# Attention with running sums: sums first, three heads fed from SBUF, and a new order of VectorE's and GpSimd's work

## The chip, the core and the metric

The kernel runs on one core of a Trainium2 chip. Its engines are named as in the profile: PE (TensorE, matrix products), PEld (its weight loads), DVE (VectorE), ACT (ScalarE), POOL (GpSimd) and SP (SyncE, which issues most of the DMAs). Each engine works through a queue of its own in order and waits on semaphores for the others. SBUF is the on-chip memory, PSUM the memory that PE writes its products to. The metric is the time of one execution on the device in microseconds (us). It is taken several times, and the median counts.

## The reference

Attention with a causal mask and a bias made of running sums, and behind it two gated MLPs whose input is the attention's output:

```python
# q, k, v: (4, 8, 576, 64), s: (4, 8, 576)
scores = (1 / sqrt(64)) * q @ k.T
cum = cumsum(maximum(s, 0), -1)
bias = -(cum[..., :, None] - cum[..., None, :])
scores = where(causal, -1e9, scores + minimum(bias, 0))
attn = exp(scores - max(scores))
attn = attn / (sum(attn) + 1e-9)
x = (attn @ v), heads side by side        # 2304 x 512
x = (sigmoid(x @ w_gate) * (x @ w_val)) @ w_out        # d_ff 1536
x = ((x @ w_a) * (x @ w_b)) @ w_out2                   # d_ff 1536
```

## The kernel before

There are 32 heads, i = 0 to 31. Each has 576 rows in 5 chunks and 64 columns. Values are split into a high part, rounded to fp32r, and a low part, the exact rest, so that products of parts come near to fp32.

**Tiles of a head.** `r` (3 buffers) holds q in one half of the partitions and k in the other. `o` (4 buffers) holds the high parts of both, and below them the rows that add the bias: the running sums `relk` and `relq`, selector rows of constants, and the row of maxima. `o2` (3 buffers) holds high and low parts for the second product. `rel` is the SBUF tile with the running sums of all heads, split in high and low. `pt` are the exponentials, `xt` the output before it is divided, `rb` the reciprocals spread over 64 partitions, `x_sb` the attention's output.

**Steps of a head, with engine and line.** Load r (SP L337). High parts: q on POOL (`hq1`, L465), k on ACT (`hk1`, L467). Copies of the high parts into `o2` by DMA: k issued by ACT (`hk2`, L468), q by SP (`hq2`, L469). Low parts by subtraction on DVE: `lok` (L470) and `loq` (L472). Loads of the head's running sums into `o` (`rel`, SP L476, L477) from DRAM copies `relk_d` and `relq_d`. Scores in two halves, S(i,0) and S(i,1) (PE L492, with the mask by L497). Both go to the same PSUM tile `ps_g`, so the second can't start before the maxima of the first, and S(i+1,0) not before those of S(i,1). Maxima on DVE (L505): `mx0` of the first half, `mx1` of the second. Their transpose on PE (mT, L512), a copy on ACT (L514) and a DMA into `o` (L516). Scores again, transposed and with the maxima taken off: ST (PE L529, L530). Exponentials on ACT (`ex`, L535). The causal cut on POOL (`cs`, three affine_selects, L551). The product with v, where columns of ones give the row sums (pv, PE L564). Copy to `xt` (ACT L573), the sums' DMA (L575), reciprocals for two heads at once (`rc`, DVE L588 and L589), their way through DRAM (`rd` L597, `rb` L594), and the final product on POOL (`xm`, L577).

**MLP weights** are split beside attention, one tile of 128x512 about every three heads: ACT L224 and L243, DVE L225, L227, L229, L232, and `wr` on POOL (L244).

**Start.** `s` is loaded, broadcast to 4 times 32 rows (L400). DVE sets tiles to constants (L346 to L356), then makes the sums (L403 to L408), ACT rounds them (`relh`, L417), DVE makes their rest (`rell`, L418). Head 0 gets its sums from SBUF: `relk` by SP (L431), `relq` by four DMAs of POOL (L424). All sums are stored to DRAM (`relq_d` by POOL L429, `relk_d` by SP L436), and heads 1 to 31 load theirs from there.

**What sets the order.** Every step is registered with `op(name, engine, cost, function, needs, prio)`. `emit(in_order=True)` takes, among the steps whose needs are already emitted, the one with the lowest `prio`. So `prio`, a time in nominal us in which a head takes HT = 6.1, sets the order of each engine's queue, and nothing else does: costs and latencies are not used, and each engine runs its queue in that order. On PE a period reads S(n,0), ST(n-2), S(n,1), pv(n-3), mT(n), S(n+1,0).

Hardware DMAs take eight semaphores in turn. A DMA waits for the one that had its semaphore before.

Of the kernel before, what the change touches and what calls it, by code (L numbers as in the profile page):

```python
# [119 lines left out]
def attn_mlp_kernel(  # L120
# [169 lines left out]
    def attention():  # L290
        with ExitStack() as c2:
# [58 lines left out]
            for e in range(2):  # L350
                nc.vector.memset(vx_t[e][:, :, (1 - e) * D:(2 - e) * D], 1.0)
                nc.vector.memset(vx_t[e][TL:128, 4, e * D:(e + 1) * D], 0.0)
            for t in nm_t:
                nc.vector.memset(t, 0.0)
            for t in pt_t:
                nc.vector.memset(t[TL:128, P0[4]:], 0.0)  # L356
# [60 lines left out]
            op("relh", "ACT", 0.67, lambda: nc.scalar.copy(out=rel[:, 0], in_=cum), ["sums"], -100)  # L417
            op("rell", "DVE", 0.7, lambda: nc.vector.tensor_tensor(  # L418
                out=rel[:, 1], in0=cum, in1=f32(rel[:, 0]), op=ALU.subtract), ["relh"], -100)


            def relq(c):
# [17 lines left out]
            for j in range(1, NO):  # L440
                if j < NR2:
                    op(("lqk", j), "SP", 0.6, lambda j=j: load_qk(j), [("sel", j - 1)], -90 + j, lat=3.0)
                op(("sel", j), "SP", 1.3, lambda j=j: selectors(o_t[j]), [("lqk", j)], -60 + j, lat=2.2)
# [374 lines left out]
```

## Time and profile before

| | |
|---|---|
| median of 3 runs | 1170.98 us (1170.71 to 1171.28) |
| the profiled execution: its own time | 1173.02 us |
| its span in the trace | 1171.3 us |
| PE busy | 1112.4 us (95%) |
| DVE busy | 648.3 us (55%) |
| ACT busy | 335.5 us (29%) |
| POOL busy | 314.5 us (27%) |
| mean granted clock of PE | 0.993 of full speed |

The span runs from the first to the last record of the trace; the execution's own time lies 1.7 us above it. The attention fills the first quarter of the span; the MLPs behind it keep PE at 90% or more of nearly every slice. Shares are means over both parts, so the shares of DVE and POOL within the attention are far above those in the table.

### The profile page before, as it was taken

What the parts mean: (1) busy time and instruction counts of PE and PEld (TensorE: products, weight loads), DVE (VectorE), ACT (ScalarE), POOL (GpSimd) and SP (SyncE); (2) the same over time, 40 slices, a digit from 0 to 9 for tenths busy, and PEclk for the clock granted to TensorE, in tenths of its full rate; (3) what the DMA queues carried; (4) which work ended last, traced back from release to release, by engine and by line L of the source; (5) the groups of instructions that cost most, each with busy time, mean ns of one, the idle gap of its engine ahead of it and who ended that gap; (6) DMA issues with size and microseconds to landing.
All of it is one profiled execution on the core that took longest, in us unless ns stands there. A gap on an engine that the chain in (4) does not pass through costs nothing.

```text
span 1171.3 us, 16041 instructions
## 1 busy us (share of the span) xinstructions
PE 1112.4 (95%) x6152; PEld 1043.9 (89%) x6152; DVE 648.3 (55%) x1016; ACT 335.5 (29%) x603; POOL 314.5 (27%) x395
## 2 busy tenths in 40 slices
PE   1799898999999999999999999999999999999998
PEld 0677777788999999999999999899999999999997
DVE  4588888846422595335873348732478333753322
ACT  1345455443322342112421123422243111321100
POOL 3146655554200242001430023311134110311100
PEclk9999999998999999999999999999999999999999
DMA  3466566723200131001220003300033000200001
GB/s 91 121 164 158 149 169 162 162 63 100 72 2 1 50 113 55 1 1 37 91 90 1 1 18 98 101 1 1 2 93 108 15 1 1 72 27 27 28 28 54
DMA packets 69730, 74.07 MB, mean 63 GB/s; under 512 B 28549, under 2 KB 53293, under 8 KB 69654
## 3 DMA queue, kind: packets, MB, share of 16 engines
q1 hardware_dynamic: 66518, 68.09, 20.3%
q10 hardware_dynamic: 2880, 4.80, 1.9%
q8 instruction: 49, 0.80, 0.3%
q14 instruction: 27, 0.22, 0.1%
q0 software_dynamic: 256, 0.15, 0.0%
HBM read 57.70 MB, written 5.60 MB: 54 GB/s over the span
## 4 chain that ended last, share of the span: by engine, by line
PE 72%; DVE 15%; DMA 4%; issue 3%; POOL 2%; ACT 2%; SPq 0%; ACTq 0%; POOLq 0%; DVEq 0%
PE ps L277 22%; PE ps L278 22%; PE ps L276 22%; PE ps_x L564 3%; DVE nm L505 3%; DVE u L227 2%; PE ps_g L492 1%; DVE raw L229 1%; DVE u L225 1%; DVE raw L232 1%; DVE o L472 1%; DMA r<-in_qk_dram 1%; POOL w L244 1%; DVE h L710 1%; DVE hf L696 1%
## 5 line engine op out<-in xcount | busy, mean ns | idle before, releaser
L276 PE MATMUL ps<-xs,w 128*128 128x384 f32 x1152 | 385.1, 334 | 0.0
L278 PE MATMUL ps<-xs,w 128*128 128x384 f32 x1152 | 385.0, 334 | 0.0
L277 PE MATMUL ps<-xs,w 128*128 128x384 f32 x1152 | 384.9, 334 | 0.0
L707 POOL TENSOR_SCALAR h<-hf 128x384 fp32r<-128x384 f32 x144 | 91.7, 637 | 577.1 <-DVE hf L696 577.1
L696 DVE TENSOR_TENSOR hf<-ps,g 128x384 f32<-128x384 f32 x144 | 79.9, 555 | 281.3 <-PE ps L278 281.2
L276 PEld LDWEIGHTS ps<-xs,w 128*128 128x128 f32 x1152 | 216.3, 188 | 0.7
L277 PEld LDWEIGHTS ps<-xs,w 128*128 128x128 f32 x1152 | 216.3, 188 | 0.7
L278 PEld LDWEIGHTS ps<-xs,w 128*128 128x128 f32 x1152 | 216.2, 188 | 0.0
L692 ACT ACTIVATE g<-ps 128x384 f32<-128x384 f32 x144 | 70.7, 491 | 437.6 <-PE ps L278 437.6
L244 POOL TENSOR_TENSOR w<-raw,w 128x512 fp32r<-128x512 f32 x72 | 100.4, 1396 | 131.8 <-ACT w L243 129.3
L710 DVE TENSOR_TENSOR h<-hf,h 128x384 fp32r<-128x384 f32 x144 | 88.9, 617 | 83.5 <-POOL h L707 83.5
L276 PE MATMUL ps<-h,w 128*128 128x384 f32 x288 | 97.9, 340 | 2.2 <-POOL h L707 2.1
L278 PE MATMUL ps<-h,w 128*128 128x384 f32 x288 | 97.6, 339 | 2.1 <-POOL w L244 2.1
L564 PE MATMUL ps_x<-pt,vx 128*128 128x320 f32 (+4 forms) x448 | 97.3, 370 | 1.1 <-ACT xt L573 0.9
L277 PE MATMUL ps<-h,w 128*128 128x384 f32 x288 | 97.6, 339 | 0.6 <-DVE h L710 0.6
L505 DVE TENSOR_REDUCE nm<-ps_g 128x1 f32<-128x512 f32 (+4 forms) x160 | 77.0, 530 | 35.0 <-PE ps_g L497 34.9
L564 PEld LDWEIGHTS ps_x<-pt,vx 128*128 128x128 f32 x448 | 77.2, 194 | 18.9 <-ACT xt L573 1.5
L277 PE MATMUL ps<-w,h 128*128 128x512 f32 x216 | 84.6, 392 | 1.0 <-POOL w L244 0.9
L278 PE MATMUL ps<-w,h 128*128 128x512 f32 x216 | 84.4, 391 | 0.0
L276 PE MATMUL ps<-w,h 128*128 128x512 f32 x216 | 84.1, 389 | 0.0
L492 PE MATMUL ps_g<-o 128*128 128x512 f32 (+2 forms) x192 | 45.9, 350 | 35.0 <-POOL o L465 18.8
L243 ACT CAST w<-raw 128x512 fp32r<-128x512 f32 x72 | 47.1, 657 | 101.5 <-DVE raw L232 95.6
(90 smaller groups left out, 1346.5 us busy)
## 6 DMA issues: line engine op xcount, KB each, us to landing
raw<-in_moe_w_out_dram SPq DMA_DIRECT2D x24, 512.0 KB
r<-in_qk_dram SPq DMA_DIRECT2D x32, 288.0 KB
raw<-in_moe_w_gate_dram SPq DMA_DIRECT2D x12, 512.0 KB
raw<-in_moe_w_val_dram SPq DMA_DIRECT2D x12, 512.0 KB
raw<-in_moe_w_a_dram SPq DMA_DIRECT2D x12, 512.0 KB
raw<-in_moe_w_b_dram SPq DMA_DIRECT2D x12, 512.0 KB
o<-o ACTq DMA_DIRECT2D x32, 144.0 KB
o<-o SPq DMA_DIRECT2D x32, 144.0 KB
```

Of the source, the lines that this page charges most:

```text
L243: ("ACT", 0.53, lambda: nc.scalar.copy(out=wtile(n, m)[:, 0], in_=value())),
L244: ("Pool", 1.23, lambda: nc.gpsimd.tensor_tensor(out=wtile(n, m)[:, 1], in0=value(), in1=f32(wtile(n, m)[:, 0]), op=ALU.subtract)),
L276: nc.tensor.matmul(out=outp, lhsT=wh, rhs=xh, start=(e == 0), stop=False)
L277: nc.tensor.matmul(out=outp, lhsT=wh, rhs=xl, start=False, stop=False)
L278: nc.tensor.matmul(out=outp, lhsT=wl, rhs=xh, start=False, stop=(e == n - 1))
L492: nc.tensor.matmul(out=ps[0:n, p0 + k0:p0 + k0 + kn], lhsT=q1[:, 128 * c:nk], rhs=k1[:, k0:k0 + kn], start=c in first or (c == 4 and k0 == ...
L505: nc.vector.tensor_reduce(out=nm[0:n, c:c + 1], in_=ps[0:n, p0:p0 + nk], axis=AX.X, op=ALU.max)
L564: nc.tensor.matmul(out=px[:, 256 + a:256 + q1_], lhsT=vx[:, j], rhs=pt[:, p0:p0 + q1_ - a], start=j == 0, stop=j == js[-1])
L692: op(("g", i, c), "ACT", 0.06 + N * 0.00083, lambda c=c, g=g: nc.scalar.activation(out=sc.get("g", (i, c))[:, 0:N], in_=sc.get("ps", g)[:, ...
L696: op(("hf", i, c), "DVE", 0.07 + N * 0.00104, lambda c=c, u=u: nc.vector.tensor_tensor(out=sc.get("hf", (i, c))[:, 0:N], in0=sc.get("ps", ...
L707: op(("hh", i, c), "Pool", 0.245 + N * 0.00083, lambda c=c, src=src: nc.gpsimd.tensor_scalar(sc.get("h", (i, c))[:, 0, 0:N], src(), 1.0, 1 ...
L710: op(("hl", i, c), "DVE", 0.07 + N * 0.00104, lambda c=c, src=src: nc.vector.tensor_tensor(out=sc.get("h", (i, c))[:, 1, 0:N], in0=src(), ...
```

## The change

The start is reordered so that `s` is loaded first and the sums are made before most of the constants. Heads 1 and 2 now get their sums from SBUF like head 0. Within a head, `loq` moves behind `mx1`, the final product `xm` moves ahead of the causal cuts, and the load of `r` for a later head is issued earlier.

```diff
-            for o in o_t:
-                nc.vector.memset(f32(o[D:2 * D]), 0.0)
             nc.vector.memset(base, 0.0)
             nc.vector.memset(zer, 0.0)
             nc.vector.memset(neg1, -1.0)
...
+            nc.vector.memset(f32(o_t[0][D:2 * D]), 0.0)
+
+            def more():
+                for t in nm_t:
+                    nc.vector.memset(t, 0.0)
+                for o in o_t[2:]:
+                    nc.vector.memset(f32(o[D:2 * D]), 0.0)
...
-            op("s", "SP", 0.5, load_s, [], -200, lat=2.3)
-            op(("lqk", 0), "SP", 0.6, lambda: load_qk(0), ["s"], -190, lat=3.0)
-            op(("sel", 0), "SP", 1.3, lambda: selectors(o_t[0]), [("lqk", 0), "selc"], -180, lat=2.2)
-            op("sums", "DVE", 2.7, sums, ["s"], -100)
...
+            op("s", "SP", 0.5, load_s, [], -300, lat=2.3)
...
+            op("ms1", "Pool", 1.2, lambda: nc.gpsimd.memset(f32(o_t[1][D:2 * D]), 0.0), ["masks"], -270)
...
+            for j in range(NR2):
+                op(("lqk", j), "SP", 0.6, lambda j=j: load_qk(j), ["s"], -290 + j, lat=3.0)
+            for j in range(2):
+                op(("sel", j), "SP", 1.3, lambda j=j: selectors(o_t[j]), [("lqk", j), "selc", "ms1"], -260 + j, lat=2.2)
+            op("sums", "DVE", 2.7, sums, ["s"], -250)
...
+            op("more", "DVE", 5.0, more, ["rell"], -219)
+            for i, (name, eng) in enumerate((("Pool", nc.gpsimd), ("ACT", nc.scalar), ("SP", nc.sync))):
+                op(("relk", i), "SP", 0.65, lambda i=i: nc.sync.dma_start(
+                    out=f32(o_t[i][D:R1, CK1:CK1 + S]), in_=f32(rel[i:NR * BH:BH])), ["rell", "more"], -210 + i, lat=2.2)
+                for c in range(NR):
+                    op(("relq", i, c), name, 0.6, lambda i=i, c=c, eng=eng: relq(eng, i, c), ["rell", "more"], -200 + i, lat=2.2)
...
+            for j in range(2, NO):
+                op(("sel", j), "SP", 1.3, lambda j=j: selectors(o_t[j]), ["more"], -180 + j, lat=2.2)
...
-                       [(w, i - NR2) for w in ("hq1", "hk1", "lok", "loq")], t0 - 3 * HT + 0.6, lat=3.0)
+                       [(w, i - NR2) for w in ("hq1", "hk1", "lok", "loq")], t0 - 4 * HT + 4.0, lat=3.0)
...
-                    out=q2[dn], in0=r[up], in1=f32(q1[up]), op=ALU.subtract), [("hq1", i)] + done2, t0 - 0.5)
+                    out=q2[dn], in0=r[up], in1=f32(q1[up]), op=ALU.subtract), [("hq1", i)] + done2, t0 - HT + 2.6)
...
-                if i:
+                if i >= NR2:
                     op(("rel", i), "SP", 0.6, rels, relst + done, t0 - 3 * HT + 2.0, lat=2.2)
...
-                    [("rb", j)], t0 + 6 * HT + 2.0)
+                    [("rb", j)], t0 + 6 * HT + 0.2)
...
-                op(("rb", j), "SP", 1.0, spread, [("rd", j), ("xm", 2 * j - 4), ("xm", 2 * j - 3)], t0 + HT + 1.0, lat=2.2)
+                op(("rb", j), "SP", 1.0, spread, [("rd", j), ("xm", 2 * j - 4), ("xm", 2 * j - 3)], t0 + HT + 0.3, lat=2.2)
...
-                weights(sc, *key, [("ST", 3 * e, 0)], HT * (3 * e + 1), at=[0, HT + 1.6, 2 * HT - 0.9, 2 * HT - 0.2, 3 * HT - 0.9, 3 * HT - 0.2, 4 * HT + 1.6, 4 * HT + 5.3])
+                weights(sc, *key, [("ST", 3 * e, 0)], HT * (3 * e + 1), at=[0, HT + 1.6, HT + 5.7, 2 * HT + 3.4, 2 * HT + 5.7, 3 * HT + 3.4, 4 * HT + 1.6, 4 * HT + 5.3])
```

Left out above: the high parts of heads 0 to 2 stand at fixed places in the start (POOL's three ahead of its DMAs), the memsets of `vx` and `pt` are in `more` too, and two steps of the later weights and of the MLP's first input are shifted alike.

On SP, behind the sums in the start, the queue of the changed kernel reads as follows. L439 and L416 bring the sums of heads 0 to 2 into `o0`, `o1`, `o2`; L445 and L447 are the stores to DRAM; L380 and L381 the selector rows; L476 is `hq2`; L483 is the first load of sums from DRAM. The waits stand in brackets.

```order
11 L439 DMA o2_186<-ya_sb_62 8x1x576 [waits DMAHW5_49,DVE_49]
...
15 L416 DMA o2_186<-ya_sb_62 2x1x144 [waits DMAHW4_49]
16 L445 DMA relk_d_239<-ya_sb_62 4x32x1152 [waits DMAHW5_49]
17 L447 DMA relq_d_240<-ya_sb_62 32x576 [waits DMAHW6_49]
18 L380 DMA o2_186<-ya_sb_62 8x1x576 [waits DMAHW7_49]
...
21 L381 DMA o3_190<-ya_sb_62 3x576 [waits DMAHW3_49]
22 L476 DMA o2_0_194<-o0_178 64x576 [waits DMAHW5_49,Pool_49]
23 L476 DMA o2_1_198<-o1_182 64x576 [waits DMAHW6_49,Pool_49]
24 L337 DMA r0_206<-in_qk_dram 128x576 [waits DMAHW7_49,DVE_49]
25 L476 DMA o2_2_202<-o2_186 64x576 [waits DMAHW0_49,Pool_49]
26 L483 DMA o3_190<-relk_d_239 8x576 [waits DMAHW2_49]
```

The selector rows of head 2 came ahead of the store before and stand behind it now; those of head 3 came behind the `hq2` of heads 0 to 2 and stand ahead of them now. `hq2` of head 0 does not read what the store writes, but its semaphore DMAHW5 is the store's; before, it had another one.

On DVE, in the steady part, a head's work between its two maxima and behind them stood like this before (L470 is `lok`, L472 `loq`, L225 to L232 the weights, L588 and L589 `rc`):

```order
L505 TENSOR_REDUCE nm3_174<-ps_g_236 128x1 x3
L225 TENSOR_SCALAR u_73<-raw_554 128x512
L472 TENSOR_TENSOR o2_0_194<-r0_206,o2_186 64x576
L227 SCALAR_TENSOR_TENSOR u_73<-raw_554,u_73 128x512
L505 TENSOR_REDUCE nm3_174<-ps_g_236 128x1
L505 TENSOR_REDUCE nm3_174<-ps_g_236 64x1
L470 TENSOR_TENSOR o2_1_198<-r1_210,o2_1_198 64x576
L588 TENSOR_SCALAR sc1_114<-sc1_114 128x9
L589 RECIPROCAL sc1_114<-sc1_114 128x9
```

and stands like this now (maxima L512, `lok` L477, `loq` L479, `rc` L595 and L596):

```order
L512 TENSOR_REDUCE nm3_174<-ps_g_222 128x1 x3
L225 TENSOR_SCALAR u_73<-raw_560 128x512
L512 TENSOR_REDUCE nm3_174<-ps_g_222 128x1
L512 TENSOR_REDUCE nm3_174<-ps_g_222 64x1
L477 TENSOR_TENSOR o2_1_198<-r1_210,o2_1_198 64x576
L479 TENSOR_TENSOR o2_1_198<-r1_210,o3_190 64x576
L595 TENSOR_SCALAR sc1_114<-sc1_114 128x9
L596 RECIPROCAL sc1_114<-sc1_114 128x9
L227 SCALAR_TENSOR_TENSOR u_73<-raw_560,u_73 128x512
```

`loq` and L227 (as L232 in the next head) have left the place between the two maxima; L225 and L229 stay there. The `loq` that follows `mx1` is now that of the same head as the `lok` before it.

On POOL, two heads of the steady part read like this before (L465 is `hq1`, L244 `wr`, L551 `cs`, L577 `xm`):

```order
L465 TENSOR_SCALAR o0_178<-r2_214 64x576
L244 TENSOR_TENSOR w0_0_65<-raw_388,w0_0_65 128x512
L551 AFFINE_SELECT pt2_134<-pt2_134 128x2x128 x2
L551 AFFINE_SELECT pt2_134<-pt2_134 64x64
L577 TENSOR_TENSOR x_sb_61<-xt0_94,rb0_86 64x576
L465 TENSOR_SCALAR o1_182<-r0_206 64x576
L551 AFFINE_SELECT pt0_126<-pt0_126 128x2x128 x2
L551 AFFINE_SELECT pt0_126<-pt0_126 64x64
L577 TENSOR_TENSOR x_sb_61<-xt1_98,rb0_86 64x576
```

and like this now (`hq1` L472, `cs` L558, `xm` L584):

```order
L472 TENSOR_SCALAR o0_178<-r2_214 64x576
L244 TENSOR_TENSOR w0_0_65<-raw_395,w0_0_65 128x512
L584 TENSOR_TENSOR x_sb_61<-xt0_94,rb0_86 64x576
L558 AFFINE_SELECT pt2_134<-pt2_134 128x2x128 x2
L558 AFFINE_SELECT pt2_134<-pt2_134 64x64
L472 TENSOR_SCALAR o1_182<-r0_206 64x576
L584 TENSOR_TENSOR x_sb_61<-xt1_98,rb0_86 64x576
L558 AFFINE_SELECT pt0_126<-pt0_126 128x2x128 x2
L558 AFFINE_SELECT pt0_126<-pt0_126 64x64
```

The product `xm` has changed places with the three cuts, so that `hq1`, now and then `wr`, and `xm` stand together.

## Rows read from the trace of the kernel before

**Rows 1.** Window of the steady stretch of attention: us, busy of each engine, PEclk, DMA share, GB/s

```profile
77.45:245.47 168.02, 153.23 (x889) 125.52 (x889) 144.80 (x235) 83.68 (x163) 96.67 (x127) 0.98 0.64 156
```

**Rows 2.** The transposes of the maxima in that stretch: duration, first and last start

```profile
L512 PE MATMUL ps_t<-idf,nm x25: 269/273/275, 77.5 to 245.5; 128*5 128x128 f32 x25
```

**Rows 3.** Timeline of DVE, one head whose maxima waited for PE

```profile
64.91 1.35 DVE L505 TENSOR_REDUCE nm<-ps_g 128x1 f32<-128x512 f32 x3
67.36 1.08 DVE L505 TENSOR_REDUCE nm<-ps_g 128x1 f32<-128x256 f32 x2 [0.31 <-PE ps_g L497]
70.93 1.35 DVE L505 TENSOR_REDUCE nm<-ps_g 128x1 f32<-128x512 f32 x3 [1.71 <-PE ps_g L497]
```

**Rows 4.** Timeline of the start: start, duration, engine, line, tiles

```profile
4.93 1.07 DVE L346 MEMSET o<- 64x1216 f32 x1 [0.20 <-issue]
8.92 0.46 DVE L403 TENSOR_SCALAR ya_sb<-ya_sb 128x576 f32<-128x576 f32 x1
12.56 0.76 DVE L418 TENSOR_TENSOR ya_sb<-ya_sb 128x576 fp32r<-128x576 f32 x1 [0.74 <-ACT ya_sb L417]
13.63 2.27 POOL L424 DMA_DIRECT2D o<-ya_sb  x4 [9.79 <-DVE ya_sb L418]
18.03 0.58 SPq L436 DMA_DIRECT2D relk_d<-ya_sb  x1
18.84 1.22 PE L492 MATMUL ps_g<-o 128*128 128x512 f32 x3 [18.84 <-POOL o L465]
29.23 0.28 SPq L476 DMA_DIRECT2D o<-relk_d  x1
31.54 1.19 PE L492 MATMUL ps_g<-o 128*128 128x512 f32 x3 [6.66 <-DMA o<-relq_d]
37.60 1.19 PE L492 MATMUL ps_g<-o 128*128 128x512 f32 x3
38.80 0.78 PE L529 MATMUL ps_e<-o 128*128 128x512 f32 x1
```

**Rows 5.** Windows of the start: GB/s and share of the DMA engines stand last

```profile
4.00:7.00 3.00, 0.00 (x0) 0.00 (x0) 2.63 (x5) 0.37 (x2) 0.00 (x0) 1.00 0.29 86
23.00:28.00 5.00, 0.70 (x3) 0.19 (x2) 1.83 (x3) 0.92 (x2) 0.00 (x0) 1.00 0.23 79
```

**Rows 6.** Lines of DVE by form, 52 to 246 us: busy, mean ns

```profile
L470 DVE TENSOR_TENSOR o<-r,o 64x576 fp32r<-64x576 f32 x28 | 33.0, 1178 | 0.9
L472 DVE TENSOR_TENSOR o<-r,o 64x576 fp32r<-64x576 f32 x28 | 28.0, 1001 | 0.9
L232 DVE SCALAR_TENSOR_TENSOR raw<-mag,raw 128x512 f32<-128x512 f32 x11 | 8.4, 768 | 0.3
L588 DVE TENSOR_SCALAR sc<-sc 128x9 f32<-128x9 f32 x13 | 3.8, 294 | 8.7 <-DMA sc<-xt 8.4
L589 DVE RECIPROCAL sc<-sc 128x9 f32<-128x9 f32 x13 | 2.8, 215 | 0.4
```

**Rows 7.** Lines of POOL by form in the same stretch

```profile
L577 POOL TENSOR_TENSOR x_sb<-xt,rb 64x576 f32<-64x576 f32 x25 | 35.6, 1425 | 1.0
L465 POOL TENSOR_SCALAR o<-r 64x576 fp32r<-64x576 f32 x27 | 20.4, 754 | 60.1 <-DMA r<-in_qk_dram 26.7 <-DVE nm L505 7.8 <-DMA rb<-rr_d 5.6
L244 POOL TENSOR_TENSOR w<-raw,w 128x512 fp32r<-128x512 f32 x8 | 10.3, 1287 | 0.0
```

**Rows 8.** Timeline of POOL and DVE about two second maxima

```profile
68.59 1.45 POOL L551 TENSOR_SCALAR_AFFINE_SELECT pt<-pt 128x256 f32<-128x256 f32 x3 [0.84 <-ACT pt L535]
81.66 1.04 POOL L551 TENSOR_SCALAR_AFFINE_SELECT pt<-pt 128x256 f32<-128x256 f32 x2
82.17 1.07 DVE L505 TENSOR_REDUCE nm<-ps_g 128x1 f32<-128x256 f32 x2
82.77 1.41 POOL L577 TENSOR_TENSOR x_sb<-xt,rb 64x576 f32<-64x576 f32 x1
83.27 1.53 DVE L470 TENSOR_TENSOR o<-r,o 64x576 fp32r<-64x576 f32 x1
```

More of the change, by code (lines that the diff above doesn't have):

```diff
@@ L349, in attention @@
             nc.vector.memset(neg1, -1.0)
[L350 to L356, printed above, removed]
+            nc.vector.memset(f32(o_t[0][D:2 * D]), 0.0)
[4 more added lines that the diff above has]
+                    nc.vector.memset(f32(o[D:2 * D]), 0.0)
+                for e in range(2):
+                    nc.vector.memset(vx_t[e][:, :, (1 - e) * D:(2 - e) * D], 1.0)
+                    nc.vector.memset(vx_t[e][TL:128, 4, e * D:(e + 1) * D], 0.0)
+                for t in pt_t:
+                    nc.vector.memset(t[TL:128, P0[4]:], 0.0)
             def selector():
@@ L408, in sums, with relq @@
                 nc.vector.tensor_scalar(cum, cum, base, SUP, ALU.subtract, ALU.mult)
-            op("selc", "Pool", 1.9, selector, [], -300)
-            op("masks", "Pool", 0.9, masks, ["selc"], -280)
-            op("mkb", "ACT", 0.7, masks_b, ["masks"], -280)
-            op("s", "SP", 0.5, load_s, [], -200, lat=2.3)
-            op(("lqk", 0), "SP", 0.6, lambda: load_qk(0), ["s"], -190, lat=3.0)
-            op(("sel", 0), "SP", 1.3, lambda: selectors(o_t[0]), [("lqk", 0), "selc"], -180, lat=2.2)
-            op("sums", "DVE", 2.7, sums, ["s"], -100)
[L417 to L422, printed above, removed]
+            def relq(eng, i, c):
                 qs = slice(SR * c, SR * (c + 1))
-                nc.gpsimd.dma_start(
-                    out=f32(o_t[0][R1:KB, CQ1 + SR * c:CQ1 + SR * (c + 1)]), in_=f32(rel[c * BH:c * BH + 1, :, qs]))
+                eng.dma_start(
+                    out=f32(o_t[i][R1:KB, CQ1 + SR * c:CQ1 + SR * (c + 1)]),
+                    in_=f32(rel[c * BH + i:c * BH + i + 1, :, qs]))
             def relq_store(c):
@@ new lines, in attention @@
+            op("mkb", "ACT", 0.7, masks_b, ["masks"], -280)
+            for j in range(NR2):
[3 more added lines that the diff above has]
+            op("sums", "DVE", 2.7, sums, ["s"], -250)
+            op("relh", "ACT", 0.67, lambda: nc.scalar.copy(out=rel[:, 0], in_=cum), ["sums"], -230)
+            op("rell", "DVE", 0.7, lambda: nc.vector.tensor_tensor(
+                out=rel[:, 1], in0=cum, in1=f32(rel[:, 0]), op=ALU.subtract), ["relh"], -220)
@@ L439, in attention @@
+            op("relz", "SP", 0.4, lambda: nc.sync.dma_start(out=relq_d[:, 2], in_=zer[0:BH]), ["rell"], -189, lat=2.5)
             relst = ["relk", "relz"] + [("rels", c) for c in range(NR)]
[L440 to L443, printed above, removed]
+            for j in range(2, NO):
+                op(("sel", j), "SP", 1.3, lambda j=j: selectors(o_t[j]), ["more"], -180 + j, lat=2.2)
@@ L508, in head @@
                     op(("S", i, g), "PE", (0.7, 0.65)[g], scores,
-                       [("rel", i), ("hq1", i), ("hk1", i), ("sel", i % NO), "mkb"] + ([("relk", 0)] + [("relq", 0, j) for j in range(NR)] if i == 0 else []),
+                       [("rel", i), ("hq1", i), ("hk1", i), ("sel", i % NO), "mkb"] + ([("relk", i)] + [("relq", i, j) for j in range(NR)] if i < NR2 else []),
                        t0 + (3.5 - 2 * HT, -HT)[g], acq=("g", (i, g)))
@@ L611, in attention @@
                 op(("x0l", k), "DVE", 0.5, lambda k=k: nc.vector.tensor_tensor(
[L612 removed]
+                    out=xs0[:, 1, k], in0=x_sb[:, k, 0:NB], in1=f32(xs0[:, 0, k]), op=ALU.subtract), [("x0h", k)], t0 + 3.5)
             sc.emit(in_order=True)
```

15 lines of the change are left out of this document (6 added, 9 removed).

## The prediction, made before the run

> **What bounds the kernel now.** I read the window of the steady stretch of attention first [rows 1]: of its 168.02 us PE is busy for 153.23 at a granted clock of 0.98 (the level of 2.4 GHz), DVE for 144.80. PE is not throttled, but neither is it closed up. The transposes of the maxima [rows 2] mark the heads: 25 starts from 77.5 to 245.5 us, so 24 periods of 168.0 / 24 = 7.00 us. The timeline of DVE about a head in which both maxima waited for PE [rows 3] shows what PE would need: from one first maxima to the next 70.93 - 64.91 = 6.02. So attention runs 0.98 us per head above its own PE rate, and DVE with POOL is where that goes. The MLPs behind it keep PE closed and aren't touched. Then I read the start [rows 4], which the change rewrites.
>
> **The start.** Before, the sums begin at 8.92, behind all memsets, and `rell` ends at 12.56 + 0.76 = 13.32; call this end R. From the first step of the sums to R it is 4.40 us. Now the sums wait for the load of s alone. When that lands I can't read directly. Between 4 and 7 us the DMAs move 86 GB/s at a share of 0.29 [rows 5], about the rate of the later store (79 GB/s at 0.23). s as loaded has 128 x 576 x 4 bytes = 295 KB; at 79 to 86 GB/s that is 3.4 to 3.7 us, and with the 2 us or so that a small DMA needs here (31.54 - 29.23 = 2.31 from issue to the matmul that waits for two of them) it lands at 6.4 if issued at 0.8. Bounds: 5.9, and 8.9, where the sums had certainly got it. POOL's three `hq1` now stand beside the sums, 0.75 us each [rows 7]; beside such work two-input DVE instructions wait (below), so I add 1.2, with bounds 0 and 2.0. R = 6.4 + 4.4 + 1.2 = 12.0, from 10.8 to 14.0.
>
> What follows R: POOL issues the four DMAs of `relq` from R + 0.31 on, 2.27 us, and landing takes 2.31: S(0,0) at R + 4.9 (before, 18.84 - 13.32 = 5.5). Heads 1 and 2 no longer wait for the way through DRAM. That wait was large: the store was issued at 18.03, the first load behind it at 29.23, so it took 11.2, and S(1,0) began at 31.54. Now S(1,0) and S(2,0) follow at the pace of scores and maxima, 37.60 - 31.54 = 6.06 each: S(2,0) at R + 17.0, ST(0) 1.2 behind it (38.80 - 37.60) at R + 18.2. The other chain to ST(0) runs through SP: the store stands behind three sets of sums, whose semaphores I expect to let it go at R + 4.7, as far behind R as before (18.03 - 13.32). `hq2` of head 0 waits for the store's semaphore, R + 4.7 + 11.2 = R + 15.9, and ST(0) gets it 2.31 to 2.5 later, R + 18.4. The two chains nearly agree, so neither needs to be exact. ST(0) at 12.0 + 18.4 = 30.4 in place of 38.80: **8.4 us gained**, 6.4 to 9.6 by the bounds of R. What follows ST(0) keeps its distance to it, since the loads behind it on SP (r of head 3, v, the weights) are released with it.
>
> **The steady part.** DVE's loop with one tile `ps_g` is mx0, S(n,1), mx1, S(n+1,0). With nothing blocked, mx0 to mx1 is 67.36 - 64.91 = 2.45, held by PE; behind mx1 (1.08 and 0.03 to the next) come `lok` and `loq` at 0.78 each, a weight step (L227 or L232) at 0.77 in two heads of three, 0.51, and half an `rc`, (0.29 + 0.22) / 2 = 0.25 [rows 6]. That is 2.45 + 1.11 + 1.56 + 0.51 + 0.25 = 5.88, under PE's 6.02. So DVE can keep PE's pace, if POOL doesn't stop it. Call the blocked time per head X; the period is 5.9 + X, not under 6.02.
>
> That POOL stops it the rows show [rows 8]: the second maxima at 82.17 last 1.07 although `xm` begins inside them at 82.77, so maxima from PSUM aren't delayed; `lok` behind them takes 1.53 and ends 0.62 after `xm`, not 0.75. In means [rows 6], `lok` takes 1.18 and `loq` 1.00 against some 0.75 unblocked: X was about 0.68 from these two. POOL has 1.43 of `xm`, 0.75 of `hq1` and 1.29 / 3 of `wr` per head [rows 7], 2.6 in all, which is X's upper end; its lower end is 0.1, all of it beside maxima.
>
> Where the block falls: it starts when the cuts of the head before are done. In the head that PE held they ended at 68.59 + 1.45 = 70.04, 2.7 behind mx1's start; in one with a late mx1 at 82.70, 0.5 behind it. In the first kind `lok` and `loq` are just through (1.11 + 1.56 = 2.67), `hq1` and `xm` (2.1) lie beside the next mx0, and only a weight step or `rc` behind `loq` is caught: two heads of three, half of them for 2.0 us, 0.67. In the second kind the block lasts to 0.5 + 2.1 = 2.6, and `lok`, due at 1.1, loses 1.5. `loq` and the weight steps that made mx1 late are gone from ahead of it, so I take two thirds of the heads for the first kind: X = 0.67 x 0.67 + 1.5 / 3 = 0.95, taken as 1.0. Period 6.9, 24 x (6.9 - 7.0) = **-2.4 us**.
>
> A rule speaks against more than that. By the Trainium skill, "SBUF — State Buffer", section "SBUF: two separate sides", the port pair that VectorE and GpSimd share is an exclusive lock: who starts first keeps it for the whole instruction, and the other fully blocks. The 1.53 of `lok` agrees. Moving work behind mx1 takes none of it off the lock, so by the rule alone nothing is gained but by order, and a longer block of `hq1`, `wr` and `xm` may even hold it longer, which is the rival below.
>
> Edits that I cost at nothing: the earlier load of r (POOL waited 26.7 us for it [rows 7], but off the path), the earlier `rb`, and one more `xm` ahead of the last head's cut (0 to 1.4, POOL is idle there).
>
> **The sum.** 1173.02 - 8.4 - 2.4 = 1162.2, for an execution like the profiled one; the median lies 2.04 below that, so **1160.2**.
>
> **Rivals.**
> (B) The block falls beside mx0 nearly always, X = 0.4, period 6.3: 24 x 0.7 = 16.8 gained, 1173.02 - 8.4 - 16.8 - 2.0 = 1145.8. For it: the 2.67 against 2.7 above. Against: `wr` makes the block 3.4 long in one head of three, and L225 and L229 still stand between the maxima. Closed up wholly (6.02) it would be 1139.
> (C) Slower. `hq1`, `wr` and `xm` run as one block with no cuts between, in the second kind of head: a late mx1 meets the block, `lok` and `loq` wait it out, the next mx1 is late again. It holds for 1.5 us, 2.8 with `wr` (1.29), so (2 x 1.5 + 2.8) / 3 = 1.9, less the 0.1 before a block ends: X = 1.8, period 7.7, +16.8: 1179.4. It is slower than before by 0.2% from X = 1.55 on (24 x 0.55 = 13.2 against 10.8 gained, and 2.3). For it: the late kind sustains itself. Against: a head held by PE ends it.
> (D) The start gains half. Nothing new stands ahead of `relq` on POOL, but the postponed memsets of DVE begin as POOL issues its DMAs. If these wait for them (4.93 to 8.92 is a like piece of memsets, 4.0), S(0,0) and all behind it come 4 us later: 1164.2. No row of before shows memsets beside POOL's DMA issues. By the Trainium skill, the same page, section "Who interferes with whom", VectorE starves GpSimd's descriptor work only in a two-port mode, which it names for copy, cast and tensor_scalar on this chip and not for memset.
>
> **Chances.** A (forecast) 0.50, B 0.20, C 0.18, D 0.12. 0.2% is 2.3 us, about what a measurement can tell from no change. A with X from 0.7 to 1.4 (6.6 to 7.3, -9.6 to +7.2 in place of -2.4) runs from 1153.0 to 1169.8; to leave out no more than 2 in 10 the range takes in half of B and part of C: 1150 to 1175. Faster: 0.40 of A, all of B, 0.08 of D: 0.68. Same, 1168.6 to 1173.3: 0.08 of A, 0.03 of C, 0.03 of D: 0.14. Slower: 0.15 of C, 0.02 of A, 0.01 of D: 0.18.
>
> **What would show it.** R at about 12, S(0,0) at 17, ST(0) at 30 in the timeline of the start; `hq2` of head 0 held until the store lands. In the steady stretch, periods near 6.9; mx0 to mx1 at about 2.5 in most heads; the means of `lok` and `loq` about 1.2 each, and weight steps behind them lengthened. The prediction is wrong if the cuts end at another place relative to mx1 than in the two heads read, so that the block always misses or always meets `lok`, or if ACT's exponentials, not DVE, set the period once `loq` is out of the way.

## The result and the profile after

The changed kernel is slower: 1181.03 us median against 1170.85 of the kernel before on the same chips, ratio 1.0092, 95% interval 1.0066 to 1.0117. The profiled execution took 1179.78 us with a span of 1177.7, 6.4 us over the span before. The forecast was 1160.2 us, with a range of 1150 to 1175.

The timeline of the start after the change (start, duration, engine, line; the lines are those of the changed kernel, as in its order excerpts):

```profile
8.49 0.46 DVE L406 TENSOR_SCALAR ya_sb<-ya_sb 128x576 f32<-128x576 f32 x1 [4.98 <-DMA ya_sb<-in_s_dram]
9.14 3.14 POOL L472 TENSOR_SCALAR o<-r 64x576 fp32r<-64x576 f32 x3 [4.13 <-DMA r<-in_qk_dram]
12.50 0.76 DVE L435 TENSOR_TENSOR ya_sb<-ya_sb 128x576 fp32r<-128x576 f32 x1 [0.74 <-ACT ya_sb L434]
17.45 1.19 PE L499 MATMUL ps_g<-o 128*128 128x512 f32 x3 [17.45 <-DMA o<-ya_sb]
18.31 0.56 SPq L445 DMA_DIRECT2D relk_d<-ya_sb  x1
29.02 1.17 SPq L476 DMA_DIRECT2D o<-o  x2
29.79 1.19 PE L499 MATMUL ps_g<-o 128*128 128x512 f32 x3 [0.31 <-DMA o<-ya_sb]
30.98 0.77 PE L536 MATMUL ps_e<-o 128*128 128x512 f32 x1
```

Here the forecast held in its end, not in its first term. The sums begin at 8.49, when s has landed, and not at 6.4. Three loads of r now run beside the load of s, as the window of the DMAs shows:

```profile
4.00:7.00 3.00, 0.00 (x0) 0.00 (x0) 0.00 (x0) 0.37 (x2) 1.00 (x1) 1.00 0.97 208
```

That is 208 GB/s at a share of 0.97, against 86 at 0.29 [rows 5]. Before, with one load of r behind it, s had landed at 7.05, by the last update of its semaphore in the trace; now that update comes at 8.47. So 1.4 of the 2.1 us that the estimate missed came with the two loads more; the rest was in the estimate itself. The sums take 13.26 - 8.49 = 4.77 with POOL's three `hq1` beside them, before 4.40. So R is 12.50 + 0.76 = 13.26, no earlier than before. But S(0,0) follows R by 4.2, S(2,0) comes 29.79 - 17.45 = 12.3 later, `hq2` of head 0 is let go at 29.02, 10.7 behind the store's issue, and ST(0) begins at 30.98 in place of 38.80 [rows 4]: 7.8 us gained, where 8.4 stood in the sum.

The steady part, by its transposes from head 3 on:

```profile
L519 PE MATMUL ps_t<-idf,nm x29: 272/273/273, 44.0 to 252.5; 128*5 128x128 f32 x29
```

28 periods in 252.5 - 44.0 = 208.5 us are 7.45 each; before, the same heads took 6.91 each. The 7.00 of [rows 2] and the 6.9 of the forecast belong to the last 24 periods, which are slower in both kernels. On that stretch the changed kernel has (252.5 - 68.6) / 24 = 7.66:

```profile
L519 PE MATMUL ps_t<-idf,nm x25: 272/273/273, 68.6 to 252.5; 128*5 128x128 f32 x25
```

From ST(0) to the last transpose it now takes 252.5 - 31.0 = 221.5 us, before 245.5 - 38.8 = 206.7: 14.8 us lost. Behind it 1177.7 - 252.5 = 925.2 us are left, before 925.8. So -7.8 + 14.8 - 0.6 = +6.4, the whole difference of the spans: the start gave what it should, and attention's steady part lost twice that.

Where in a head? One head of the changed kernel, DVE and POOL in one timeline:

```profile
82.14 1.08 DVE L512 TENSOR_REDUCE nm<-ps_g 128x1 f32<-128x256 f32 x2 [1.10 <-PE ps_g L504]
82.29 1.07 POOL L558 TENSOR_SCALAR_AFFINE_SELECT pt<-pt 128x256 f32<-128x256 f32 x3 [0.69 <-ACT pt L542]
83.25 0.76 DVE L477 TENSOR_TENSOR o<-r,o 64x576 fp32r<-64x576 f32 x1
83.82 0.71 POOL L472 TENSOR_SCALAR o<-r 64x576 fp32r<-64x576 f32 x1 [0.47 <-DMA r<-in_qk_dram]
84.03 2.38 DVE L479 TENSOR_TENSOR o<-r,o 64x576 fp32r<-64x576 f32 x1
84.51 1.30 POOL L244 TENSOR_TENSOR w<-raw,w 128x512 fp32r<-128x512 f32 x1
85.88 1.85 POOL L584 TENSOR_TENSOR x_sb<-xt,rb 64x576 f32<-64x576 f32 x1
86.45 1.31 DVE L595 TENSOR_SCALAR sc<-sc 128x9 f32<-128x9 f32 x1
87.93 1.29 DVE L512 TENSOR_REDUCE nm<-ps_g 128x1 f32<-128x512 f32 x3
90.26 1.08 DVE L512 TENSOR_REDUCE nm<-ps_g 128x1 f32<-128x256 f32 x2 [0.65 <-PE ps_g L504]
```

The cuts (L558) end at 83.36, 1.2 behind the start of the second maxima. `hq1` (L472), `wr` (L244) and `xm` (L584) run from 83.82 to 87.73 as one block, and all that DVE has behind `lok` in that time is caught: `loq` (L479) 2.38 for 0.75, `rc` (L595) 1.31 for 0.17. From mx1 to the next mx0 it takes 87.93 - 82.14 = 5.79 us; in the head of before that PE held it was 3.57 [rows 3]. Behind that mx0 DVE has one weight step and then waits 0.65 for PE. This head is one of the long ones. Over heads 8 to 30 of the timelines, mx1 to the next mx0 takes 5.08 on average and mx0 to mx1 2.54; before, it was 3.47 and 3.55.

In the lines by form, 52 to 246 us, the blocked time has moved from `lok` to `loq`, the weight step and `rc`:

```profile
L479 DVE TENSOR_TENSOR o<-r,o 64x576 fp32r<-64x576 f32 x26 | 31.9, 1229 | 0.8
L477 DVE TENSOR_TENSOR o<-r,o 64x576 fp32r<-64x576 f32 x26 | 22.6, 871 | 0.8
L227 DVE SCALAR_TENSOR_TENSOR u<-raw,u 128x512 int32<-128x512 int32 x9 | 11.2, 1247 | 0.2
L595 DVE TENSOR_SCALAR sc<-sc 128x9 f32<-128x9 f32 x13 | 9.2, 708 | 2.9 <-DMA sc<-xt 2.6
```

Before, `lok` took 1178, `loq` 1001, L227 886 and `rc`'s first half 294 ns (L227 in the same view of before; the others in [rows 6]). `lok` and `loq` together lose 22.6 + 31.9 - 52 x 0.75 = 15.5 us, 0.60 a head, a little less than the 0.68 before; L227 and `rc` lose more than before.

The waits, 52 to 246 us, after (what waited, for whom, us in total, times, the longest):

```profile
DVE nm L512 <- PE ps_g L504: 25.5, 29, 2.3
PE ps_g L499 <- DVE nm L512: 22.0, 14, 2.7
POOL o L472 <- DMA r<-in_qk_dram: 18.7, 10, 3.1
```

and before:

```profile
DVE nm L505 <- PE ps_g L497: 12.8, 17, 1.7
PE ps_g L492 <- DVE nm L505: 6.6, 10, 1.7
PE ps_t L512 <- DVE nm L505: 5.0, 6, 1.3
```

DVE now waits 25.5 us for PE's scores and PE 22.0 us for DVE's maxima. Each waits for the other in turn: PE behind the long stretch, DVE in the short one.

### The profile page after: what moved, and what is told of

Read it like the earlier page. It is cut to its first block, busy times and chain, and to the rows that moved or that the text cites. A ratio compares the mean times of both kernels' runs of the same rounds, so it can differ in the third digit from the quotient of the medians.

```text
span 1177.7 us, 16046 instructions
## 1 busy us (share of the span) xinstructions
PE 1115.5 (95%) x6152; PEld 1045.4 (89%) x6152; DVE 658.3 (56%) x1015; ACT 334.8 (28%) x603; POOL 314.5 (27%) x396
## 4 chain that ended last, share of the span: by engine, by line
PE 75%; DVE 15%; DMA 3%; issue 3%; POOL 2%; ACT 1%; ACTq 1%; SPq 0%; POOLq 0%; DVEq 0%
PE ps L277 22%; PE ps L278 22%; PE ps L276 22%; PE ps_x L571 5%; DVE nm L512 2%; DVE u L227 2%; PE ps_g L499 2%; DVE o L479 1%; DMA sc<-xt 1%; DVE raw L232 1%; DVE raw L229 1%; DVE h L717 1%; DVE o L477 1%; DVE hf L703 1%; POOL w L244 1%
## 5 line engine op out<-in xcount | busy, mean ns | idle before, releaser
L244 POOL TENSOR_TENSOR w<-raw,w 128x512 fp32r<-128x512 f32 x72 | 100.0, 1390 | 131.8 <-ACT w L243 129.3
L571 PE MATMUL ps_x<-pt,vx 128*128 128x320 f32 (+4 forms) x448 | 103.9, 387 | 1.1 <-POOL pt L558 0.8
L571 PEld LDWEIGHTS ps_x<-pt,vx 128*128 128x128 f32 x448 | 81.5, 204 | 21.3 <-issue 5.2
L512 DVE TENSOR_REDUCE nm<-ps_g 128x1 f32<-128x512 f32 (+4 forms) x160 | 77.6, 534 | 38.1 <-PE ps_g L504 38.0
```

Of the source, the lines that this page charges most:

```text
L244: ("Pool", 1.23, lambda: nc.gpsimd.tensor_tensor(out=wtile(n, m)[:, 1], in0=value(), in1=f32(wtile(n, m)[:, 0]), op=ALU.subtract)),
L512: nc.vector.tensor_reduce(out=nm[0:n, c:c + 1], in_=ps[0:n, p0:p0 + nk], axis=AX.X, op=ALU.max)
L571: nc.tensor.matmul(out=px[:, 256 + a:256 + q1_], lhsT=vx[:, j], rhs=pt[:, p0:p0 + q1_ - a], start=j == 0, stop=j == js[-1])
```

## The experiments

Four pieces of the steady part were undone or made alone, always with the new start. Against the changed kernel, the piece undone reads:

```diff
# loq
-("hq1", i)] + done2, t0 - HT + 2.6)
+("hq1", i)] + done2, t0 - 0.5)
# weight steps (both lists)
-at=[0, HT + 1.6, HT + 5.7, 2 * HT + 3.4, 2 * HT + 5.7, 3 * HT + 3.4, ...
+at=[0, HT + 1.6, 2 * HT - 0.9, 2 * HT - 0.2, 3 * HT - 0.9, 3 * HT - 0.2, ...
# xm, with rb
-("rb", j)], t0 + 6 * HT + 0.2)
+("rb", j)], t0 + 6 * HT + 2.0)
-... t0 + HT + 0.3, lat=2.2)
+... t0 + HT + 1.0, lat=2.2)
# load of r
-("hq1", "hk1", "lok", "loq")], t0 - 4 * HT + 4.0, lat=3.0)
+("hq1", "hk1", "lok", "loq")], t0 - 3 * HT + 0.6, lat=3.0)
```

Each ratio is against the kernel before on the same chip. "new" is the place of the changed kernel. The period is that between transposes from head 2 to 31 (of the changed kernel from head 3). It comes from the one profiled execution; in e2_xm and e4_w that was the fastest of twelve, 5.5 and 6.2 us under the median, so there the ratio tells more. In the runs that start from the old places (e1, g1, h1, h2, h3, i1, j2) one step of the MLP's first input is back at its old place too.

| run | loq | weights | xm, rb | load of r | ratio [95%] | period, us |
|---|---|---|---|---|---|---|
| kernel before, with the old start | old | old | old | old | 1 | 6.94 |
| changed kernel | new | new | new | new | 1.0092 [1.0066, 1.0117] | 7.45 |
| e1_start | old | old | old | old | 0.9933 [0.9907, 0.9960] | 6.79 |
| e2_xm | new | new | old | new | 1.0010 [0.9990, 1.0030] | 7.10 |
| e3_loq | old | new | new | new | 0.9914 [0.9892, 0.9936] | 6.73 |
| e4_w | new | old | new | new | 1.0052 [1.0033, 1.0071] | 7.12 |
| i2_lqk_back | new | new | new | old | 0.9965 [0.9951, 0.9978] | 6.97 |
| g1_loq_alone | new | old | old | old | 0.9933 [0.9909, 0.9958] | 6.77 |
| h2_w_alone | old | new | old | old | 0.9963 [0.9950, 0.9977] | 6.87 |
| h3_xm_alone | old | old | new | old | 1.0016 [0.9999, 1.0032] | 7.03 |
| i1_lqk_alone | old | old | old | new | 0.9949 [0.9929, 0.9969] | 6.82 |
| h1_loq_w | new | new | old | old | 0.9963 [0.9947, 0.9980] | 6.87 |
| g4_loq_w | old | old | new | new | 1.0022 [1.0001, 1.0043] | 7.02 |
| i3_w_xm | old | new | new | old | 0.9963 [0.9947, 0.9979] | 6.82 |

**First round.** e1_start:

> 

> The new start with all the old places in the steady part (loq, xm, rb, the load of r, the weight steps). Both theories below expect ST(0) at 31 us and a period of about 7.0 us between transposes, so 1171 - 7.8 = 1163 us. If the start's gain is given back by mT(31), as a rival has it (the heads only queue up behind something that the start doesn't move), it takes 1171.

0.67% faster, about the 7.8 us of the start. The start is sound and nothing takes it back. e2_xm, e3_loq and e4_w:

> 

> The changed kernel with xm and rb back at their old places, xm behind the three cuts. Theory 1 (hq1, wr and xm stand as one block that begins when the cuts end, about 1.2 us behind the start of the second maxima, and stops lok, loq, rc and the weight step): the block is broken up, the period falls from 7.45 to 6.5 to 7.0, and the time to 1155 to 1169 us. Theory 2 (loq, moved, makes DVE's half behind the second maxima too long, wherever POOL's work stands): the period stays above 7.3, 1177 to 1182 us.

> 

> The changed kernel with loq back ahead of the second maxima of the next head. Theory 1: the block stays and meets lok, rc and the weight steps, and a loq ahead of mx1 is in the way again: 1173 to 1182 us, period 7.2 to 7.5. Theory 2: the half behind the second maxima is short again, period 6.9 to 7.0, 1161 to 1166 us.

> 

> The changed kernel with the weight steps L227 and L232 back ahead of the second maxima. Theory 1: the weight steps are only one of the things caught, and ahead of mx1 they delay it: 1174 to 1182 us. Theory 3 (the weight steps behind loq are what is caught, so their place is the cause): period 6.9 or less, under 1167 us.

All three undo some of the loss, but `loq` alone put back undoes all of it and more: 1160.45 us, a little under what theory 2 had (1161 to 1166), and the period of 6.73 is under its 6.9 to 7.0. e2_xm lies between both theories, and e4_w fits theory 1.

**Second round**, on theory 4, which came out of that (what stands between the maxima is free).

> 

> The new start, all the old places in the steady part, and loq alone moved behind the second maxima. Theory 4 (between its two maxima DVE must wait for PE's second scores anyway, about 1 us a head; loq stood in that wait for nothing, and behind mx1 it costs its own time in a loop that DVE sets): against the 1161.9 us and the period of 6.79 of the start alone the period rises by 0.4 to 0.7, to 7.2 to 7.5, and the time to 1173 to 1182 us. Theory 1 (the block of hq1, wr and xm is the cause; here xm is at its old place and there is no such block): period 6.7 to 6.9, 1159 to 1165 us.

0.9933 [0.9909, 0.9958], the same as the start alone, as theory 1 had it. So `loq` behind the second maxima costs nothing by itself; theory 4 in this form, and theory 2, fell. On average the move takes mx0 to mx1 from 3.61 to 2.85 and mx1 to mx0 from 3.29 to 3.99: what one stretch gives up, the other takes on.

> 

> The changed kernel with loq and the weight steps back ahead of the second maxima; what stays new is the start, xm ahead of the cuts, the earlier rb and the earlier load of r. Theory 4: with loq in DVE's wait the rest moves little, 1155 to 1164 us. Theory 1 (xm's place ahead of the cuts is what costs): 1168 to 1178 us.

1.0022, 0.9% over the start alone, as theory 1 had it, although `loq` stands between the maxima. `loq`'s place is neither enough for a loss nor needed for one.

> 

> The changed kernel with loq back ahead of the next head's second maxima and lok moved there too. Theory 4: lok fills the rest of DVE's wait between the maxima, period 6.4 to 6.7 in place of 6.75, 1151 to 1160 us. If the wait is used up by loq already, or the transposed scores wait for the later lok: period 6.8 or more, 1161 to 1172 us.

The edit puts `lok` at `t0 - 0.7`, beside `loq`: 1.0046 [1.0026, 1.0066], and at 1172.84 us just above both its ranges. mx0 to mx1 grows to 4.47 on average, and mx1 to mx0 shrinks to 2.87. Crowding the stretch ahead of the second maxima loses as crowding the one behind them does.

> 

> The changed kernel with the high part of q made on ACT instead of POOL from head 3 on, so that POOL's two-input and one-input work beside lok and loq is a third shorter. If the time that DVE stands blocked by POOL sets the period together with the lost wait (theory 4 with the blocked time): period 7.45 falls by 0.3 to 0.7, 1160 to 1173 us. If it is the order on DVE alone: 1177 to 1182 us. If ACT's exponentials now come late by the 0.67 us that it has more to do, the time lies above 1182 us.

```diff
-nc.gpsimd.tensor_scalar(q1[up], r[up], 1.0, 1.0, ALU.mult, ALU.mult)
+... if i < NR2 else nc.scalar.copy(out=q1[up], in_=r[up])
```

1.0051 [1.0032, 1.0071] against 1.0092, with a period of 7.17: a shorter block helps, by less than expected.

**Third round**, the pieces apart.

> 

> The new start with xm, rb and the load of r at their old places, and loq and the weight steps L227 and L232 both moved behind the second maxima. Theory 5 (DVE has two stretches per head, mx0 to mx1 and mx1 to the next mx0; each hides as much DVE work as PE has beside it, and loq and the weight steps behind mx1 leave the first one empty and the second too long): period 7.0 to 7.3 in place of 6.8, 1165 to 1175 us against 1160 for loq alone. Theory 1 in its last form (xm ahead of the cuts, or the earlier load of r, is what costs): period 6.8, 1157 to 1163 us.

> 

> The new start with everything at its old place but the weight steps L227 and L232, which stand behind the second maxima. Theory 5: loq fills the first stretch, the weight steps go into the second, the stretches are as even as in the run with loq back: period 6.7 to 6.85, 1155 to 1162 us. If the weight steps cost behind mx1 by themselves: 1166 us or more.

> 

> The new start with everything at its old place but xm and rb, so that xm stands ahead of the cuts. If xm's place costs by itself (the cuts, and with them the product with v, wait behind xm, which waits for the reciprocals' DMA): 1166 to 1173 us, period 7.0 or more. If it is the earlier load of r that made the run with loq and the weight steps back slow: 1158 to 1164 us, as the start alone.

h1's time, 1165.02 us, is at the edge of theory 5's range, and its period of 6.87 is nearer to theory 1's 6.8; h2, at 1163.68 us, falls between its two ranges. h1 and h2 have the same ratio, 0.9963, so `loq` adds nothing to the weight steps either, which speaks against theory 5 in the form of h1 (work of DVE alone). h3 is 0.8% over the start alone: of the single pieces, only `xm` ahead of the cuts clearly costs.

> 

> The changed kernel with a memset of 128x576 added on DVE behind the first maxima of every head, 0.54 us each; it computes nothing that is used. Theory 5: the first stretch has about 1.05 us in which DVE waits for PE's second scores, the memset lies in it, and the time stays within 1178 to 1186 us although DVE has 32 x 0.54 = 17 us more to do. If DVE's sum of work sets the period: 1192 to 1200 us.

```diff
+op(("dum", i), "DVE", 0.5, lambda: nc.vector.memset(zer, 0.0), [("mx", i, 0)], t0 + 4.4 - 2 * HT)
```

1184.00 us, ratio 1.0138 [1.0110, 1.0165], 0.5% over the changed kernel. But the edit had a side effect that the expectation did not have: `zer` is read by a store of the start, and the first memset waited for it, as its timeline shows (with a head of the steady part):

```profile
29.38 0.54 DVE L519 MEMSET ya_sb<- 128x576 f32 x1 [8.83 <-DMA o<-ya_sb]
83.57 0.54 DVE L519 MEMSET ya_sb<- 128x576 f32 x1
84.54 1.08 DVE L512 TENSOR_REDUCE nm<-ps_g 128x1 f32<-128x256 f32 x2 [0.43 <-PE ps_g L504]
```

That held the start up by 30.9 - 23.1 = 7.8 us (equal to the start's gain by chance), as the first transposes of this kernel and of the changed one show:

```profile
L520 PE MATMUL ps_t<-idf,nm x32: 269/273/374, 30.9 to 254.5; 128*5 128x128 f32 x32
```

```profile
L519 PE MATMUL ps_t<-idf,nm x32: 269/273/374, 23.1 to 252.5; 128*5 128x128 f32 x32
```

From there 31 periods are 7.21 us each, against 7.40 in the changed kernel. So 17 us more of DVE work between the maxima cost nothing in the steady part: that stretch holds a wait in the changed kernel, as theories 4 and 5 say. DVE's mean wait ahead of mx1 falls from 0.65 to 0.22 us.

**Fourth round**, on what was still open.

> 

> The new start with everything at its old place but the load of r, which is issued earlier. If the shares of the edits add up (loq 0, weight steps +0.3%, xm with rb +0.8%, so +0.5% is left for the load of r out of +1.6%): 1166 to 1169 us in place of 1162. If the load of r only matters with loq behind the second maxima: 1159 to 1164 us.

> 

> The changed kernel with the load of r alone back at its old place. If the shares add up: 0.5% under the changed kernel, 1171 to 1176 us. If the load of r does nothing: 1178 to 1182 us.

> 

> The new start, with xm, rb and the weight steps moved, loq and the load of r at their old places. The run with loq back was the fastest so far, against the sum of the shares (+0.8 and +0.3%). If the weight steps and xm suit each other: 1156 to 1164 us, period 6.8. If the shares add up, 1170 to 1176 us, and the earlier load of r was what made that run fast.

> 

> The changed kernel with one small instruction more on POOL ahead of hq1 from head 4 on, a copy of 128x1 of the first maxima just made, so that hq1, wr and xm can't start before these maxima are there and fall beside the wait for the second scores and the second maxima. Theory 5 (where the block falls makes the period): blocked time behind the second maxima falls from 1.1 to 0.5 us a head or less, period 6.6 to 7.0 in place of 7.45, 1156 to 1169 us. If only the order on DVE counts: 1177 to 1185 us. If the cuts, which now wait for the block, become late for the product with v: over 1185 us, with PE waiting for POOL.

i1 is not to be told from the start alone, and neither is i3 (1164.08 us, at the edge of its first range). i2 takes back 1.3%, more than either of its ranges had: the load of r, whose place changes no order on DVE or POOL, decides whether the other three pieces together lose. The timeline of i2 shows how (lines as in the changed kernel):

```profile
81.67 0.66 POOL L472 TENSOR_SCALAR o<-r 64x576 fp32r<-64x576 f32 x1 [5.42 <-DMA r<-in_qk_dram]
82.31 1.42 POOL L584 TENSOR_TENSOR x_sb<-xt,rb 64x576 f32<-64x576 f32 x1
82.58 1.08 DVE L512 TENSOR_REDUCE nm<-ps_g 128x1 f32<-128x256 f32 x2 [1.10 <-PE ps_g L504]
83.68 1.98 POOL L558 TENSOR_SCALAR_AFFINE_SELECT pt<-pt 128x256 f32<-128x256 f32 x3
83.69 1.00 DVE L477 TENSOR_TENSOR o<-r,o 64x576 fp32r<-64x576 f32 x1
84.72 0.84 DVE L479 TENSOR_TENSOR o<-r,o 64x576 fp32r<-64x576 f32 x1
85.60 0.17 DVE L595 TENSOR_SCALAR sc<-sc 128x9 f32<-128x9 f32 x1
86.15 1.35 DVE L512 TENSOR_REDUCE nm<-ps_g 128x1 f32<-128x512 f32 x3
```

and its waits, 50 to 225 us:

```profile
POOL o L472 <- DMA r<-in_qk_dram: 39.3, 16, 5.5
PE ps_g L499 <- DVE nm L512: 11.0, 11, 2.3
```

`hq1` begins at 81.67, when r lands, 0.9 ahead of the second maxima, and `xm` ends at 83.73, just as `lok` begins. In the head of the changed kernel r landed 0.47 us behind the cuts, and `hq1` ran 1.7 behind the start of the second maxima; in all, POOL waited 18.7 us for r there in place of 39.3. The heads shown are no exceptions in this. Over heads 8 to 30, `hq1` starts ahead of the second maxima in none of 22 cases in the changed kernel and behind their end in 19; in i2 it starts ahead of them in 15 of 23 and behind them in one.

Why the same load does nothing in i1 and e3, the traces show too. A load of r needs its buffer, which `loq` of three heads before must have left. With `loq` at its old place that one ends about 0.9 us ahead of mx1, and the load is issued 0.2 to 0.4 behind mx1 (e3, i1), not much before the 0.7 of the old place (e1). With `loq` moved, `loq` is through 4.3 ahead of mx1, and the load goes out 2.0 ahead of it in the changed kernel, against 1.6 behind it in i2. So the two edits work together.

i4 does by force what the late load does by chance:

```diff
+if i > NR2:
+    op(("gate", i), "Pool", 0.1, lambda: nc.gpsimd.tensor_scalar(
+        gt[:, 0:1], nm_t[(i - 1) % 4][:, 0:1], 1.0, 1.0, ALU.mult, ALU.mult), [("mx", i - 1, 0)], t0 - 3 * HT + 5.1)
```

Its timeline (the small copy is L476, `hq1` L473, `xm` L588, `lok` L481, `loq` L483, maxima L516):

```profile
97.84 0.19 POOL L476 TENSOR_SCALAR gt<-nm 128x1 f32<-128x1 f32 x1 [2.06 <-DVE nm L516]
97.99 0.66 POOL L473 TENSOR_SCALAR o<-r 64x576 fp32r<-64x576 f32 x1
98.73 1.08 DVE L516 TENSOR_REDUCE nm<-ps_g 128x1 f32<-128x256 f32 x2 [1.05 <-PE ps_g L508]
98.73 1.42 POOL L588 TENSOR_TENSOR x_sb<-xt,rb 64x576 f32<-64x576 f32 x1
99.84 0.92 DVE L481 TENSOR_TENSOR o<-r,o 64x576 fp32r<-64x576 f32 x1
100.80 0.84 DVE L483 TENSOR_TENSOR o<-r,o 64x576 fp32r<-64x576 f32 x1
102.31 1.35 DVE L516 TENSOR_REDUCE nm<-ps_g 128x1 f32<-128x512 f32 x3 [0.67 <-PE ps_g L508]
```

`hq1` and `xm` lie beside the wait of DVE and the second maxima, which last 1.08 as always. `lok` loses 0.17, `loq` 0.09, and mx1 to mx0 is 102.31 - 98.73 = 3.58. Its ratio is 0.9967 [0.9949, 0.9986], 1.25% under the changed kernel, period 6.98: on both engines the order of the changed kernel, and r loaded early as there, with POOL made to wait. `hq1` starts ahead of the second maxima in all 23 heads. So it is the place of the block and not the load itself that costs.

This head and that of i2 are among the best of theirs. In the means, 52 to 232 us, `lok` and `loq` lose no less than the 0.60 a head of the changed kernel: 0.74 in i2 and 0.67 in i4. What is won lies behind them, `rc`'s first half at 323 and 211 ns in place of 708, L227 at 739 and 711 in place of 1247. Counting all that DVE does behind mx1, above the shortest time of its kind, the blocked time is 0.66 us a head before, 1.35 in the changed kernel, 0.95 in i2 and 0.88 in i4, which is less of a fall than i4's expectation had.

**Last round.**

> 

> The changed kernel with POOL held until the first maxima are made (as in i4) and the high part of q made on ACT from head 3 on, so that the held block is xm alone, with wr in one head of three. If lok caught by the block's end is what is left: xm ends about 0.7 us behind the start of the second maxima, lok is free, blocked time falls from 0.7 to 0.3 us a head, period 6.3 to 6.7 in place of 7.03, 1146 to 1157 us. If DVE's second stretch is too long by its own work: period 6.8 or more, 1159 to 1166 us. If ACT is late with the exponentials: over 1166 us.

> 

> The new start with everything at its old place, and the high part of q made on ACT from head 3 on. Less POOL work to be caught by: period 6.5 to 6.8 in place of 6.84, 1152 to 1161 us. If ACT's extra 0.67 us delays the exponentials as much: 1161 to 1168 us.

j1 joins i4 and g2: 0.9962 [0.9943, 0.9982], period 6.76. j2 joins e1 and g2: 0.9960 [0.9940, 0.9980], period 6.94. Both times lie in the second range of their expectations, and neither beats what it was built on. j1's profile has a shorter period, but its median is that of i4; j2's second stretch is longer (3.84 against 3.29 on average). That ACT has more to do ahead of its exponentials may be why; no run tried it.

The best of all is e3_loq: the changed kernel with `loq` back, 1160.45 us, 0.86% under the kernel before [0.64, 1.08]. That it beats e1 and g1 (0.9933 both) is within the intervals. Its window of the steady part (us, busy times of PE, PEld, DVE, ACT, POOL, then the granted clock), before it that of the changed kernel:

```profile
50.00:225.00 175.00, 150.40 (x870) 123.25 (x868) 148.69 (x227) 81.44 (x160) 89.43 (x122) 0.96 0.59 148
```

```profile
50.00:225.00 175.00, 161.68 (x951) 131.97 (x950) 157.88 (x251) 90.76 (x176) 102.47 (x133) 1.00 0.64 162
```

and its waits of PE in the same stretch:

```profile
PE ps_g L499 <- DVE nm L512: 7.5, 14, 1.5
PE ps_t L519 <- DVE nm L512: 4.6, 7, 1.7
```

PE waits 12.1 us for maxima in place of 22.0, and in 175 us it runs 951 matmul instructions in place of 870. The blocked time has hardly gone, 1.40 a head in both stretches against 1.67, but the stretches are even, 3.45 and 3.35, and DVE waits 0.21 a head for scores in place of 0.99.

## Why the prediction was wrong

- **The start** was right in its sum: 7.8 us for 8.4, and e1_start, which has it alone, is faster by about as much. Its terms were off and partly cancel, which is luck: s came 2.1 later than estimated (8.49), the 1.2 for `hq1` beside the sums was 0.4, and the way from R to ST(0) was 0.7 shorter. R, at 13.26, lay within its bounds. That the gain comes from heads 1 and 2 no longer waiting for DRAM was right.
- **The step that failed** is "Edits that I cost at nothing: the earlier load of r (POOL waited 26.7 us for it [rows 7], but off the path)". Together with the other pieces it costs 1.3% (1.0092 to 0.9965 in i2). Without it the forecast comes out nearly: the period is 7.07 on the stretch of the forecast's 6.9, and the ratio 0.9965 where 1160.2 us stand for 0.991. The wait for r was off the path, but it held POOL's block back to the maxima, where it blocks nothing. Taken away, the block moved onto `loq`, the weight step and `rc`.
- With it fell the step **where the block falls**: I read from two heads of before that the cuts end 2.7 or 0.5 behind mx1, and took two thirds of the heads for the first. Over heads 8 to 30 the cuts end 2.5 or more behind mx1 in 9 of 23 already before, and in 4 of 23 in the changed kernel; the head shown has 1.2. Nor does the block start with their end: `hq1` waits for r, or for others, until it starts 1.9 behind mx1 on average, where it mostly misses `lok` and meets `loq` and all behind it. The prediction named another place of the cuts as a sign that it is wrong.
- **The size of X** was 1.0 in the forecast. On the forecast's own stretch it was 7.66 - 5.88 = 1.78. Of that, about 1.35 is blocked time behind mx1, 0.34 are waits for PE ahead of mx0, and mx0 to mx1 is 0.09 longer than the sum had it (means over heads 8 to 30). So a part is not blocked time: a mean of X does not show heads in which DVE is early and waits for PE, and such a head gives nothing back to the next one. DVE's waits for scores went from 12.8 us in 28 heads to 25.5 in 26, 0.46 to 0.98 a head.
- **The DVE sum** of 5.88 counted mx0 to mx1 as a fixed 2.45, which is nearly right in the changed kernel (2.54). What it hid: before, that stretch took 3.55, filled with `loq` and weight steps, and DVE waited only 0.09 in it; now 0.65 of it is a wait, and h4_dummy shows that it is free room.
- **Rival C** named the place (one block that stops `lok` and `loq`) and gave a period of 7.7 and 1179.4 us; 7.66 and 1181.0 were measured. It had 0.18. It put the loss on `lok` and `loq`, though; these lose no more than before, and what came to it lies on `rc`, the weight steps and the waits. Its argument against, that a head held by PE ends the late kind, did not hold: in the changed kernel the second maxima do wait for PE, 16.8 of the 25.5 us by their lines, and the block still comes behind them.
- **Rival D** did not happen: POOL issued its four DMAs in 2.28 us beside the postponed memsets, before 2.27 [rows 4]. The prediction's "Nothing new stands ahead of `relq` on POOL" was wrong, as the three `hq1` do, but they were done at 12.28, ahead of R. **Rival B** did not happen either.

What stays open: why `xm` ahead of the cuts costs 0.8% when moved alone (h3) and nothing clear with the weight steps (i3). In h3 `hq1` and `xm` start ahead of mx1 in most heads, where `loq` and the weight steps then stand, and mx0 to mx1 grows to 4.05; in i3, without the weight steps there, it is 3.14. That is the likely reason, but no run holds the block fixed for these two. Nor do the runs part the places of `hq1` and `xm`: in the changed kernel `xm` also waits 25.2 us for `rb` (52 to 246 us), in i2 hardly at all, and a late `xm` catches what stands late behind mx1. The granted clock is 0.96 of full speed (2.4 GHz) in the changed kernel's steady window and 1.00 in e3's; i2 has 0.96 too at 1.3% less time, so the clock doesn't carry what i2 takes back, but its share in the rest was not measured.
